# Sliding-window attention with a rational feed-forward: the order of all instructions planned by a list scheduler in the source

## Chip, cores and metric

The kernel runs on one core of one Trainium2 chip. The metric is the device time of one execution in microseconds (us), lower is better. Times named "span" run from the first to the last instruction of one profiled execution.

A core has five engines with a queue of instructions each: PE (matrix products, results into PSUM), DVE (vector operations), ACT (activation functions, copies), POOL (elementwise operations on SBUF) and SP (here it issues the DMAs). Each engine takes the instructions of its queue strictly in order; an instruction that waits for a semaphore holds all that stand behind it.

## What is computed

```python
# q, k, v: (8, 8, 576, 64);  window 64, scale 1/8
scores = scale * np.matmul(q, k.transpose(0, 1, 3, 2))
mask = (rel >= 0) & (rel < window)          # rel = row - column
attn = softmax(np.where(mask, scores, -1e9))
x = np.matmul(attn, v)                       # to (4608, 512)
h = x @ w_in                                 # w_in (512, 2048)
P = a[0] + a[1] * h + a[2] * h**2 + a[3] * h**3
Q = 1.0 + np.abs(b[0]) * np.abs(h) + np.abs(b[1]) * h**2
out = (P / (Q + 1e-6)) @ w_out               # w_out (2048, 512)
```

All in float32. The weights arrive as 8-byte words and are decoded on the chip.

## The kernel before

**Tiling.** The 4608 tokens are cut into 12 chunks of 384 (CH). The 2048 hidden columns are cut into 16 tiles of 128. A step (c, i) handles hidden tile i of chunk c; there are 192 steps. Each float32 product is split into three products of a shorter format (high and low parts of weights and data).

**A step** has an f1 product, `ffn1` up to L258: 4 blocks of the model width times 3 products, 12 matmuls of 128x384 into an `h` buffer of PSUM (2 buffers). Then the gate, L265 to L278: ACT makes `ah`, `num`, `u` from h; DVE multiplies `num` by h twice (L268, L269, the last readers of h); POOL multiplies `u` by `ah` (L270); ACT takes logarithm and exponential for 1/Q (L273, L274); DVE makes the high part `gh` and, with three more operations, the low part `gl` (L275 to L278). So DVE has six operations a gate, ACT five, POOL one. The temporaries `ah`, `u`, `num` have 2 buffers each, `gh` and `gl` four (LAG + 1). Last comes the output product, `ffn2`, L298: 9 matmuls of 128x512 into the three accumulators o0, o1, o2 of the chunk, issued LAG = 3 steps after the f1 product.

**Phases.** Steps run as chunk 0 tiles 0 to 7, chunk 1 tiles 0 to 7, chunk 1 tiles 8 to 15, chunk 0 tiles 8 to 15, and then chunks 2 to 11 with all 16 tiles. The first half of chunk 0's output is parked in `part` (L305) and added in L310.

**Weights.** `decode` (L110 to L133) turns one 512 KB tile into its high and low part: a DMA into `w_st` (3 buffers), ACT (L124), POOL (L127), DVE (L128, L129), ACT (L132), DVE (L133), with `w_c` in 2 buffers. There are 16 tiles of w_in and 16 of w_out.

**Attention.** Each chunk has four units, one for each pair of heads. `unit_load` issues the DMAs of q, k, v (L160 to L166); `unit_scores` makes the scores on PE (L200, 24 small matmuls; for chunks 1 and 2, PEM, the mask is added on PE, L193), masks on DVE (L211), takes the maximum (L207 or L214), exponentials on ACT (L218 or L221, six each with its sum), the reciprocal of the sums on DVE (L223, L224), and the normalisation (L225), on DVE for chunk 0 and on POOL for the others. `unit_transpose` transposes on PE (L232) into the same single PSUM tile `ps_s` that the scores use, and ACT copies to `pT` (L234). `unit_av` multiplies with v on PE (L243) into `ps_x` and makes the parts xh (ACT, L248) and xl (DVE, L249) of x, the input of the f1 products. q, kt, vt and `sm` have 2 buffers each.

**What sets the order.** The source emits the prologue (the four units of chunk 0 with four tiles of w_in between them), and then, step by step, the decodes due at that step, the f1 product and gate, the attention calls due, and the output product of three steps before. Tables say at which step a decode or a unit is due: the units of a chunk are spread over the phase ahead of it. This emission order is only a priority: the tile framework reorders the instructions with its own scheduler and cost model (`schedule_with_timeline_sim=True`) before it fixes each engine's queue.

Of the kernel before, what the change touches and what calls it, by code (L numbers as in the profile page):

```python
# [26 lines left out]
QADD = 1.0 + 1e-6  # L27


@with_exitstack  # L30
def swa_rational_ffn(ctx: ExitStack, tc: tile.TileContext, qT, kT, v, w_in, w_out, a, b, out):
# [121 lines left out]
    def unit_load(c, hp):  # L153
        q = kv.tile([P, TC, WIN], F32, name="q")
        kt = kv.tile([P, TC + 1, WIN], F32, name="kt")
        vt = kv.tile([P, TC, P], F32, name="vt")
        kw, vw, first = [], [], None
        j = kb = vb = 0
        for bi, t0, n in segments(c):
            nc.sync.dma_start(out=q[:, j:j + n, :].rearrange("p t s -> p (t s)"),  # L160
                              in_=qT[bi, hp, :, t0 * WIN:(t0 + n) * WIN])
            k0 = max(t0 - 1, 0)
            nw = n if t0 else n - 1
            nc.sync.dma_start(out=kt[:, kb:kb + nw + 1, :].rearrange("p t s -> p (t s)"),
                              in_=kT[bi, hp, :, k0 * WIN:(k0 + nw + 1) * WIN])
# [12 lines left out]
        m0 = None if first is None else MASKS[first]
        live[c, hp] = dict(q=q, kt=kt, vt=vt, kw=kw, vw=vw, m0=m0)

    def unit_scores(c, hp):
        u = live[c, hp]

        ps = ps_a.tile([P, 2, 512], F32, name="ps_s", bufs=1)
        m0 = u["m0"]
        on_pe = c in PEM
        if m0 is None:
            mm = mask[:, 1:2, :].broadcast_to([P, PR, P])
        else:
            mm = mask[:, m0:m0 + PR, :]  # L190
        if on_pe:
            for z in range(2):
                nc.tensor.matmul(ps[:, z, 0:PR * P].rearrange("p (r c) -> p r c", c=P), ident_r, mm, start=True, stop=False)  # L193
        for p in range(PR):
            for z in range(2):
                for e in range(2):
                    j = 2 * p + e
                    k = u["kt"][z * 64:z * 64 + 64].rearrange("p t s -> p (t s)")
                    w = u["kw"][j] * WIN
                    nc.tensor.matmul(ps[e * 64:e * 64 + 64, z, p * P:(p + 1) * P], u["q"][z * 64:z * 64 + 64, j, :],  # L200
                                     k[:, w:w + P], start=not on_pe, stop=not on_pe or p == PR - 1)
        sm = att.tile([P, 2 * PR, P], F32, name="sm")
        NR = 2 * PR
        nmx = att.tile([P, NR], F32, name="nmx")
        if on_pe:
            pss = ps[:, :, 0:PR * P].rearrange("p z (r c) -> p z r c", c=P)
            nc.vector.tensor_reduce(out=nmx.rearrange("p (z r) -> p z r", z=2), in_=pss, axis=AX.X, op=ALU.max, negate=True)  # L207
            nc.vector.scalar_tensor_tensor(out=nmx, in0=nmx, scalar=SCALE, in1=zero, op0=ALU.mult, op1=ALU.add)
        else:
            for z in range(2):  # L210
                nc.vector.scalar_tensor_tensor(out=sm[:, z * PR:(z + 1) * PR, :],  # L211
                                               in0=ps[:, z, 0:PR * P].rearrange("p (r c) -> p r c", c=P), scalar=SCALE,
                                               in1=mm.bitcast(F32), op0=ALU.mult, op1=ALU.add)
            nc.vector.tensor_reduce(out=nmx, in_=sm, axis=AX.X, op=ALU.max, negate=True)  # L214
        sums = att.tile([P, NR], F32, name="sums")
        for j in range(NR):
            if on_pe:
                nc.scalar.activation(sm[:, j, :], ps[:, j // PR, (j % PR) * P:(j % PR + 1) * P], AF.Exp, scale=SCALE,  # L218
                                     bias=nmx[:, j:j + 1], accum_out=sums[:, j:j + 1])
            else:  # L220
                nc.scalar.activation(sm[:, j, :], sm[:, j, :], AF.Exp, bias=nmx[:, j:j + 1], accum_out=sums[:, j:j + 1])  # L221
        rs = att.tile([P, NR], F32, name="rs")
        nc.vector.scalar_tensor_tensor(out=sums, in0=sums, scalar=1e-9, in1=zero, op0=ALU.add, op1=ALU.add)  # L223
        nc.vector.reciprocal(out=rs, in_=sums)  # L224
        (nc.vector if c < 1 else nc.gpsimd).tensor_tensor(out=sm, in0=sm, in1=rs.unsqueeze(2).broadcast_to([P, NR, P]), op=ALU.mult)  # L225
        u["sm"] = sm

    def unit_transpose(c, hp):
        u = live[c, hp]
        ps = ps_a.tile([P, 2, 512], F32, name="ps_s", bufs=1)  # L230
        for j in range(2 * PR):
            nc.tensor.transpose(ps[:, j // PR, (j % PR) * P:(j % PR + 1) * P], u["sm"][:, j, :], ident)  # L232
        pT = att.tile([P, 2, PR * P], F32, name="pT", bufs=1)
        nc.scalar.copy(out=pT, in_=ps[:, :, 0:PR * P])  # L234
        u["pT"] = pT

    def unit_av(c, hp):
        u = live.pop((c, hp))

        ps = ps_a.tile([P, TC, WIN], F32, name="ps_x", bufs=1)  # L240
        for j in range(TC):
            for z in range(2):
                nc.tensor.matmul(ps[z * 64:z * 64 + 64, j, :], u["vt"][:, u["vw"][j], z * 64:z * 64 + 64],  # L243
                                 u["pT"][:, z, j * WIN:(j + 1) * WIN], start=True, stop=True)
        xh[c, hp] = xp.tile([P, CH], F32R, name=f"xh{hp}")
        xl[c, hp] = xp.tile([P, CH], F32R, name=f"xl{hp}")
        x = ps.rearrange("p t s -> p (t s)")
        nc.scalar.copy(out=xh[c, hp], in_=x)  # L248
        nc.vector.tensor_tensor(out=xl[c, hp], in0=x, in1=xh[c, hp].bitcast(F32), op=ALU.subtract)  # L249

    gs = {}

    def ffn1(c, i):
        h = ps_h.tile([P, CH], F32, name="h")
        n = 0
        for cc in range(NCC):
            for w, x in ((wi_h, xl), (wi_h, xh), (wi_l, xh)):
                nc.tensor.matmul(h, w[:, cc, i * P:(i + 1) * P], x[c, cc], start=n == 0, stop=n == 3 * NCC - 1)  # L258
# [150 lines left out]
```

## Time and profile before

| what | value |
|---|---|
| median of 3 runs | 1013.71 us (1013.44 to 1014.66) |
| span of the profiled execution | 1014.7 us |
| busy: PE, DVE, ACT, POOL | 94%, 81%, 71%, 32% of the span |
| PE, DVE busy in 0 to 175 us | 120.9 us, 153.3 us |
| PE busy in 175 to 1000 us | 825.0 us |
| mean granted TensorE clock | 0.971 |

How to read the lines. In the busy time by stretch, each row gives the stretch, its length, and for each engine the busy time and the number of instructions in brackets; then the granted TensorE clock (1.00 is full speed), the busy share of the DMA engines and GB/s. In the groups of instructions, a row gives the source line, engine, operation, output and inputs, shapes, count, busy time in us and mean ns of one, and after the bar the idle time of the engine ahead of them with what ended it. In the order of time, a row gives start and duration in us; a bracket at its end names the idle time before it and what released it. PEld is the weight load of PE.

### The profile page before, as it was taken

How to read it: one execution, taken by the hardware profiler on the slowest of the kernel's cores; microseconds unless marked ns; L12 is line 12 of the kernel's file. 1: busy time of each engine (PE TensorE's matmuls, PEld its weight loads, DVE VectorE, ACT ScalarE, POOL GpSimd, SP SyncE). 2: the span in 40 equal slices, each digit the busy share in tenths (PEclk: the TensorE clock that was granted, in tenths of full speed). 3: DMA queues.
4: the chain of work that ended last, by engine and by line, in shares of the span. 5: the costliest groups of instructions: out<-in, count | busy, mean ns of one | idle time of the engine just before them, and what ended most of it. 6: DMA issues, size and time to landing. Idle time of an engine off the chain costs nothing.

```text
span 1014.7 us, 18277 instructions
## 1 busy us (share of the span) xinstructions
PE 954.8 (94%) x6640; PEld 844.8 (83%) x6640; DVE 825.9 (81%) x1539; ACT 725.1 (71%) x1735; POOL 324.9 (32%) x283
## 2 busy tenths in 40 slices
PE   3688578999999999999999999999999999999997
PEld 2576367989898888898888888888988988988996
DVE  7899788878888788788788787787787888787885
ACT  5777666667676777877777777777777777777664
POOL 4566544223332222223223223223223223222221
PEclk9679789999999999999999999999999999999999
DMA  7634630021211211210211211110121111100000
GB/s 239 221 110 138 207 98 16 1 77 29 90 31 31 83 42 34 88 37 29 76 46 31 67 58 34 64 61 29 61 61 31 62 63 35 64 17 1 32 1 31
DMA packets 37817, 64.09 MB, mean 63 GB/s; under 512 B 4448, under 2 KB 24928, under 8 KB 37728
## 3 DMA queue, kind: packets, MB, share of 16 engines
q1 hardware_dynamic: 37728, 62.93, 19.4%
q8 instruction: 52, 0.85, 0.4%
q14 instruction: 37, 0.30, 0.1%
HBM read 53.48 MB, written 9.44 MB: 62 GB/s over the span
## 4 chain that ended last, share of the span: by engine, by line
PE 84%; DVE 10%; ACT 3%; issue 2%; POOL 1%; DMA 1%; SPq 0%; POOLq 0%; DVEq 0%
PE h L258 38%; PE o L298 37%; PE ps_x L243 3%; PE ps_s L200 3%; PE ps_s L232 3%; DVE w_c L128 2%; POOL w_st L127 1%; DVE w_c L129 1%; DVE wo_l L133 1%; DVE num L277 1%; DVE u L276 1%; DVE wi_l L133 1%; DVE gh L275 1%; DMA w_st<-w_in 1%; ACT w_c L124 0%
## 5 line engine op out<-in xcount | busy, mean ns | idle before, releaser
L270 POOL TENSOR_TENSOR u<-u,ah 128x384 f32<-128x384 f32 x192 | 198.2, 1033 | 383.3 <-ACT u L267 343.7
L258 PE MATMUL h<-xl,wi_h 128*128 128x384 f32 x768 | 267.5, 348 | 20.3 <-DVE num L269 18.6
L258 PE MATMUL h<-xh,wi_h 128*128 128x384 f32 x768 | 262.7, 342 | 0.0
L258 PE MATMUL h<-xh,wi_l 128*128 128x384 f32 x768 | 262.5, 342 | 0.0
L298 PE MATMUL o<-wo_h,gl 128*128 128x512 f32 x576 | 233.5, 405 | 7.2 <-DVE gl L278 7.2
L298 PE MATMUL o<-wo_h,gh 128*128 128x512 f32 x576 | 228.3, 396 | 0.0
L298 PE MATMUL o<-wo_l,gh 128*128 128x512 f32 x576 | 227.0, 394 | 0.0
L268 DVE TENSOR_TENSOR num<-num,h 128x384 f32<-128x384 f32 x192 | 106.2, 554 | 111.9 <-ACT num L266 111.5
L265 ACT ACTIVATE ah<-h 128x384 f32<-128x384 f32 x192 | 94.5, 492 | 124.1 <-PE h L258 84.9
L258 PEld LDWEIGHTS h<-xl,wi_h 128*128 128x128 f32 x768 | 147.3, 192 | 27.8 <-DVE num L269 20.7
L258 PEld LDWEIGHTS h<-xh,wi_h 128*128 128x128 f32 x768 | 147.4, 192 | 4.8
L225 POOL TENSOR_TENSOR sm<-sm,rs 128x768 f32<-128x768 f32 x44 | 68.4, 1555 | 253.2 <-DVE rs L224 250.5
L258 PEld LDWEIGHTS h<-xh,wi_l 128*128 128x128 f32 x768 | 147.0, 191 | 0.6 <-issue 0.2
L275 DVE SCALAR_TENSOR_TENSOR gh<-num,a_sb,ah 128x384 fp32r<-128x384 f32 x192 | 119.3, 633 | 28.4 <-ACT ah L274 28.3
L298 PEld LDWEIGHTS o<-wo_h,gl 128*128 128x128 f32 x576 | 109.0, 189 | 33.7 <-DVE gl L278 8.8
L267 ACT ACTIVATE u<-ah,b_sb 128x384 f32<-128x384 f32 x192 | 135.6, 707 | 0.0
L221 ACT ACTIVATE sm<-sm,nmx 128x128 f32<-128x128 f32 x240 | 93.3, 390 | 57.4 <-DVE nmx L214 57.4
L298 PEld LDWEIGHTS o<-wo_h,gh 128*128 128x128 f32 x576 | 109.3, 190 | 25.2
L266 ACT ACTIVATE num<-h,a_sb 128x384 f32<-128x384 f32 x192 | 128.3, 668 | 0.0
L298 PEld LDWEIGHTS o<-wo_l,gh 128*128 128x128 f32 x576 | 109.2, 190 | 18.5
L269 DVE SCALAR_TENSOR_TENSOR num<-num,a_sb,h 128x384 f32<-128x384 f32 x192 | 117.7, 614 | 6.1
L277 DVE SCALAR_TENSOR_TENSOR num<-num,a_sb,u 128x384 f32<-128x384 f32 x192 | 116.7, 622 | 0.4
(52 smaller groups left out, 1139.2 us busy)
## 6 DMA issues: line engine op xcount, KB each, us to landing
out<-ob SPq DMA_DIRECT2D x33, 256.0 KB, 2.5
w_st<-w_in SPq DMA_DIRECT2D x16, 512.0 KB, 3.7
w_st<-w_out SPq DMA_DIRECT2D x16, 512.0 KB, 4.2
q<-qT SPq DMA_DIRECT2D x32, 192.0 KB, 3.2
vt<-v SPq DMA_DIRECT2D x16, 384.0 KB, 3.1
vt<-v SPq DMA_DIRECT2D x16, 320.0 KB, 3.0
kt<-kT SPq DMA_DIRECT2D x16, 224.0 KB, 3.6
kt<-kT SPq DMA_DIRECT2D x16, 192.0 KB, 3.4
```

Source lines behind the costliest of these rows:

```text
L221: nc.scalar.activation(sm[:, j, :], sm[:, j, :], AF.Exp, bias=nmx[:, j:j + 1], accum_out=sums[:, j:j + 1])
L225: (nc.vector if c < 1 else nc.gpsimd).tensor_tensor(out=sm, in0=sm, in1=rs.unsqueeze(2).broadcast_to([P, NR, P]), op=ALU.mult)
L258: nc.tensor.matmul(h, w[:, cc, i * P:(i + 1) * P], x[c, cc], start=n == 0, stop=n == 3 * NCC - 1)
L265: nc.scalar.activation(ah, h, AF.Abs)
L266: nc.scalar.activation(num, h, AF.Identity, scale=a_sb[:, 3:4], bias=a_sb[:, 2:3])
L267: nc.scalar.activation(u, ah, AF.Identity, scale=b_sb[:, 1:2], bias=b_sb[:, 0:1])
L268: nc.vector.tensor_tensor(out=num, in0=num, in1=h, op=ALU.mult)
L269: nc.vector.scalar_tensor_tensor(out=num, in0=num, scalar=a_sb[:, 1:2], in1=h, op0=ALU.add, op1=ALU.mult)
L270: nc.gpsimd.tensor_tensor(out=u, in0=u, in1=ah, op=ALU.mult)
L275: nc.vector.scalar_tensor_tensor(out=gh, in0=num, scalar=a_sb[:, 0:1], in1=ah, op0=ALU.add, op1=ALU.mult)
L277: nc.vector.scalar_tensor_tensor(out=num, in0=num, scalar=a_sb[:, 0:1], in1=u, op0=ALU.add, op1=ALU.subtract)
L298: nc.tensor.matmul(acc[c][t], g[:, ts], w[:, i, :], start=first and n == 0, stop=last and n == 2)
```

## The change

The functions above are taken apart into operations, each a small function bound to one engine, with a planned cost, a rank, the operations it comes after, and the buffer slots it uses. A class `Plan` holds them all. Its method `order` simulates the five engines: again and again it takes, over all engines, the operation that can start earliest, and among those of one engine that can start within 0.02 us of one another the one of lowest rank. A handover between engines costs 0.15 us in the plan. A buffer slot is free when its last user has ended. The operations are then emitted in the order of their planned starts, inside `tc.manual_schedule()`, so that the framework keeps this order.

What the diff changes beside that:

- Ranks: a unit of chunk 0 has -12 to -9, a unit of another chunk the step at which its phase's predecessor begins plus a quarter phase for each unit, minus AHEAD = 3; w_in tile i has the step that first needs it minus 1.5, a w_out tile that step plus LAG minus 1.5; a gate its step; an output product its step plus LAG + 0.5.
- Units are tied to one another only kind by kind (scores after scores, transposes after transposes, values after values).
- q and k are loaded by one operation, v by another.
- The normalisation of chunk 0 moves from DVE to POOL.
- x has two fixed sets of buffers, and a chunk's x waits for the last f1 product of the set's former holder.
- The last outputs go through the `w_st` buffers instead of `part`.
- The loads of the coefficients a and b are emitted ahead of everything in the plan.

```diff
+class Plan:
+    LATENCY = 0.15
...
+    def order(self):
...
+            for e in ENGINES:
+                able = []
+                for op in ready[e]:
+                    if any(not slots[s.pool] for s in op.takes):
+                        continue
+                    t = max([free[e], op.ready] + [min(slots[s.pool]) for s in op.takes])
+                    able.append((t, op))
...
+                t0 = min(t for t, _ in able)
+                t, op = min(((t, op) for t, op in able if t <= t0 + 0.02), key=lambda x: (x[1].rank, x[0]))
+                if best is None or t < best[0]:
+                    best = t, op
...
+        return sorted(self.ops, key=lambda o: o.start)
...
+    plan = Plan({"w_st": 3, "w_c": 2, "qk": 2, "vt": 2, "sm": 2, "pT": 1, "ps_s": 1, "ps_x": 1, "h": 2, "tmp": 2, "gp": LAG + 1,
+                 "o0": 1, "o1": 1, "o2": 1, "x": NCH})
...
+        o = plan.add("SP", 2.3, rank - 2, load, uses=[st])
+        o = plan.add("ACT", 0.57, rank, scale, [o], [st, sc])
+        o = plan.add("POOL" if pool_sign else "ACT", 1.8 if pool_sign else 0.57, rank, sign, [o], [st])
+        o = plan.add("DVE", 0.62, rank, put_sign, [o], [st, sc])
+        o = plan.add("DVE", 0.62, rank, put_low, [o], [st, sc])
+        o = plan.add("ACT", 0.56, rank, high, [o], [sc])
+        return plan.add("DVE", 0.62, rank, rest, [o], [sc])
...
+        r = lambda n: rank + 0.03 * n
+        o = link("load_qk", plan.add("SP", 1.9, r(0) - 2, load_qk, [], [sqk]))
+        lv = link("load_v", plan.add("SP", 1.8, r(0) - 1.9, load_v, [], [svt]))
+        o = link("scores", plan.add("PE", 1.36 if on_pe else 1.0, r(1), scores, [o, chain.get("scores")], [sqk, ssm, sps]))
+        if not on_pe:
             for z in range(2):
+                o = plan.add("DVE", 0.47, r(2), lambda z=z: masked(z), [o], [ssm, sps])
+        o = plan.add("DVE", 1.15 if on_pe else 0.87, r(3), maxima, [o], [ssm, sps] if on_pe else [ssm])
+        o = plan.add("ACT", 2.1, r(4), exps, [o], [ssm, sps] if on_pe else [ssm])
+        o = plan.add("DVE", 0.45, r(5), invert, [o])
+        o = plan.add("POOL", 1.6, r(6), normalise, [o], [ssm])
+        o = link("transposes", plan.add("PE", 0.7, r(7), transposes, [o, chain.get("transposes")], [ssm, spt]))
+        o = plan.add("ACT", 0.75, r(8), copy_pT, [o], [spt, spT])
+        o = plan.add("PE", 0.95, r(9), values, [o, lv, chain.get("values")], [svt, spT, spx])
...
+        r = lambda n: s + 0.05 * n
+        f = f1[s] = plan.add("PE", 2.09, s, products, x_ready[c] + [tile_in[i], f1.get(s - 1)], [sh])
+        a0 = plan.add("ACT", 0.42, r(1), absolute, [f], [sh, st])
+        n0 = plan.add("ACT", 0.58, r(2), num0, [a0], [sh, st])
+        u_0 = plan.add("ACT", 0.61, r(3), u0, [a0], [st])
+        n1 = plan.add("DVE", 0.47, r(4), num1, [n0], [sh, st])
+        n2 = plan.add("DVE", 0.53, r(5), num2, [n1], [sh, st])
+        u_1 = plan.add("POOL", 1.05, r(5), u1, [u_0], [st])
...
+        g = plan.add("DVE", 0.54, r(8), g_high, [o, n2], [st, sg])
+        o = plan.add("DVE", 0.5, r(9), product, [g], [st, sg])
+        o = plan.add("DVE", 0.53, r(10), remainder, [o], [st])
+        gate_done[s] = plan.add("DVE", 0.47, r(11), g_low, [o], [st, sg])
...
+            o = plan.add("PE", 0.695, s + LAG + 0.5 + 0.01 * t, lambda t=t: products(t),
+                         [gate_done[s], tile_out[i], f2.get((s - 1, t)), f2.get((s, t - 1))], [sg, so[t]])
...
+        tile_in[i] = plan_decode(w_in[i], wi_h[:, :, sl], wi_l[:, :, sl], need[i] - 1.5, True)
+        tile_out[i] = plan_decode(w_out_v[:, i, :], wo_h[:, i, :], wo_l[:, i, :], need[i] + LAG - 1.5, True)
...
+                order.append((c, k, -12 + k if c == 0 else before + (prev // NU) * k - AHEAD))
...
+    load_coefficients()
+    with tc.manual_schedule():
+        for op in plan.order():
+            op.emit()
```

More of the change, by code (lines that the diff above doesn't have):

```diff
@@ L30, in swa_rational_ffn @@
+ENGINES = "PE", "DVE", "ACT", "POOL", "SP"
 @with_exitstack
@@ L228, in unit_transpose @@
[L228 to L249, printed above, removed]
@@ L291, in ffn2 @@
         last = s == total - 1 or steps[s + 1][0] != c
+        d, sg = gs.pop(s)
         if first:
-            acc[c] = [ps_o.tile([P, DO], F32, name=f"o{t}") for t in range(NTS)]
-        gh, gl = gs.pop((c, i))
-        for t in range(NTS):
-            ts = slice(t * P, (t + 1) * P)
-            for n, (g, w) in enumerate(((gl, wo_h), (gh, wo_l), (gh, wo_h))):
-                nc.tensor.matmul(acc[c][t], g[:, ts], w[:, i, :], start=first and n == 0, stop=last and n == 2)
-        if not last:
-            return
@@ new lines, in products, with store @@
+        def products(t):
+            if first:
+                acc[t] = ps_o.tile([P, DO], F32, name=f"o{t}")
+            ts = slice(t * P, (t + 1) * P)
+            for n, (g, w) in enumerate(((d["gl"], wo_h), (d["gh"], wo_l), (d["gh"], wo_h))):
+                nc.tensor.matmul(acc[t], g[:, ts], w[:, i, :], start=first and n == 0, stop=last and n == 2)
+        def store(t, e):
+            if spill:
+                if t == 0:
+                    part[c] = const.tile([P, NTS, DO], F32, name=f"part{c}")
+                nc.scalar.copy(out=part[c][:, t, :], in_=acc[t])
+                return
+            ob = e["ob"] = stage.tile([P, DO], F32, name="ob", tag="w_st", bufs=3)
+            if merge:
+                nc.vector.tensor_tensor(out=ob, in0=acc[t], in1=part[c][:, t, :], op=ALU.add)
+            else:
+                nc.scalar.copy(out=ob, in_=acc[t])
@@ new lines, in swa_rational_ffn @@
+    seen = []
+    for c, i0, i1 in phases:
+        if c not in seen:
+            before = begin[c] - prev
+            for k in range(NU):
+                order.append((c, k, -12 + k if c == 0 else before + (prev // NU) * k - AHEAD))
+            seen.append(c)
+        prev = i1 - i0
+    last_step = {}
+    for s, (c, i) in enumerate(steps):
+        last_step[c] = s
+    holder = {}
+    n = 0
+    s = 0
+    for c, k, rank in order:
+        if c >= C0 and k == 0:
+            old = max(x for x in range(c) if slot_of[x] == slot_of[c])
+            while s <= last_step[old]:
+                plan_gate(s)
+                s += 1
+            free_x[c] = [f1[last_step[old]]]
+        plan_unit(c, k, rank)
```

461 lines of the change are left out of this document (296 added, 165 removed).

## The prediction

> **What bounds the kernel now.** I read the page first, then busy time by stretch, then the f1 products by stretch, then the waits of the first 175 us, and the order of time in three places.
>
> ```profile
> span 1014.7 us, 18277 instructions
> PE 954.8 (94%) x6640; PEld 844.8 (83%) x6640; DVE 825.9 (81%) x1539; ACT 725.1 (71%) x1735; POOL 324.9 (32%) x283
> ```
> ```profile
> core 0: us, PE busy (x) PEld busy (x) DVE busy (x) ACT busy (x) POOL busy (x), PEclk, DMA share, GB/s
> 0.00:25.00 25.00, 8.51 (x108) 6.67 (x108) 17.46 (x32) 13.59 (x41) 11.42 (x20) 0.99 0.73 237
> 25.00:100.00 75.00, 58.02 (x416) 49.26 (x417) 71.50 (x117) 55.67 (x141) 43.88 (x26) 0.80 0.51 161
> 100.00:125.00 25.00, 14.25 (x136) 10.84 (x134) 19.91 (x34) 14.92 (x35) 13.84 (x8) 0.77 0.61 189
> 125.00:175.00 50.00, 40.15 (x233) 34.49 (x234) 44.44 (x74) 34.26 (x89) 23.68 (x17) 0.88 0.22 69
> 175.00:1000.00 825.00, 825.00 (x5720) 737.23 (x5719) 667.46 (x1278) 602.25 (x1426) 231.07 (x212) 1.00 0.14 45
> ```
>
> There are three stages. From 175 to 1000 us PE is busy for all 825 us: whatever the order of the other engines, nothing is to be won there, only lost. Before 175 us PE works 8.5 + 58.0 + 14.3 + 40.2 = 120.9 us and idles 54.1, part of it at a low granted clock; DVE works 17.5 + 71.5 + 19.9 + 44.4 = 153.3 us and idles 21.7. So DVE bounds the start. What follows 1000 us is taken up in part 3. The end is the moment at which PE is saturated plus the PE work left then. The position of PE at the start is counted by f1 products (12 matmuls a step), that of DVE by the gh operation (one a step):
>
> ```profile
> 0.00:175.00 175.00, 50.05 (x204) 44.34 (x204) 0.84 0.47 149
> 175.00:203.00 28.00, 15.21 (x83) 14.70 (x84) 1.00 0.00 1
> ...
> 0.00:175.00 175.00, 11.79 (x15) 0.84 0.47 149
> 175.00:203.00 28.00, 4.95 (x8) 1.00 0.00 1
> ```
>
> The first two rows are line L258, the last two L275. At 175 us PE has done 204/12 = 17 products, at 203 us (204 + 83)/12 = 24, with 15 and 23 gates behind them. Yet all 32 weight tiles are decoded by 175 us (the L129 row below), although the second half of w_in is first needed from step 16 to step 23, one tile a step. The scheduler of before filled DVE with decodes ahead of their need, and what PE needed came late. Its worst place is around 110 us:
>
> ```profile
> 107.00 0.69 DVE L133 SCALAR_TENSOR_TENSOR wi_l<-w_c,wi_h 128x512 fp32r<-128x512 f32 x1
> ...
> 111.91 1.96 DVE L129 SCALAR_TENSOR_TENSOR w_c<-w_st,w_c 128x512 uint32<-128x512 uint32 x1
> 111.61 1.72 POOL L225 TENSOR_TENSOR sm<-sm,rs 128x768 f32<-128x768 f32 x1 [1.52 <-DVE rs L224]
> 113.38 0.90 PE L232 MATMUL ps_s<-ident,sm 128*128 128x128 f32 x3 [5.37 <-POOL sm L225]
> ```
>
> PE waits 5.4 us for the last attention unit of chunk 1, without which step 8 cannot be computed, while DVE decodes tiles. The waits of the first 175 us say the same of the gates (total, times, longest): a product waits for an h buffer that DVE has not yet read.
>
> ```profile
> PEld h L258 <- DVE num L269: 20.7, 7, 6.2
> ```
>
> **Part 1, the order of the start (gain).** The number of instructions does not change, and phases and steps are the same (eight steps of chunk 0, eight of chunk 1, then the second halves). What changes is who goes first. Units of chunk 0 get ranks -12 to -9, units of chunk 1 -3 to 3, a w_in tile the step that needs it minus 1.5, a w_out tile plus 1.5, a gate its step. So attention goes ahead of decodes, and a decode goes ahead of a gate only when it is due. To bring PE to step 24 the DVE needs, beside the 153.3 us of the first 175, eight more gates (15 to 23).
>
> ```profile
> L129 DVE SCALAR_TENSOR_TENSOR w_c<-w_st,w_c 128x512 uint32<-128x512 uint32 x32 | 26.0, 814 | 0.2
> L275 DVE SCALAR_TENSOR_TENSOR gh<-num,a_sb,ah 128x384 fp32r<-128x384 f32 x15 | 11.8, 786 | 3.1 <-ACT ah L274 3.0
> L268 DVE TENSOR_TENSOR num<-num,h 128x384 f32<-128x384 f32 x17 | 9.2, 545 | 0.7 <-ACT num L266 0.7
> L225 DVE TENSOR_TENSOR sm<-sm,rs 128x768 f32<-128x768 f32 x4 | 4.3, 1070 | 0.1
> ```
>
> A gate has six DVE operations; these are the longest and the shortest, 786 and 545 ns, so a gate costs between 6 x 0.545 = 3.3 and 6 x 0.666 = 4.0 us; durations overlap a little at their ends, so I take 3.5: 28 us. The four normalisations of chunk 0 (L225, 4.3 us) leave DVE for POOL. They don't leave it free: beside the POOL row at 111.61 the DVE operation at 111.91 took 1.96 us where its like at 107.00 took 0.69. Four such blocks cost 4 x 1.3 = 5 us, so the move is worth between -4.3 and +0.7 us; I take -2, since a block needs a two-input operation just behind it. POOL itself has room (43.9 us busy of 75). DVE then needs 153.3 + 28 - 2 = 179 us, and step 24 comes at 179 plus the DVE idle time. If idle stays at 21.7, that is 201 us against 203: a gain of 2. The first 25 us alone hold 25 - 17.5 = 7.5 us, the wait for the first loads and scores, and they can't go: 186.5, a gain of 16. I take 12 us: always the most urgent of the ready operations goes, so DVE should seldom be without one, but the plan's prices lie below the rows (0.47 to 0.54 us for a gate's operations, 0.62 for the decode's 0.81), and a queue that runs behind its plan waits. That is 191 us, **gain 12**. The two coefficient loads now stand ahead of the first q on SP's queue and not behind the second w_st; at 0.7 us an issue (below) the first scores come up to 1.4 us later, which I leave within those 12.
>
> ```profile
> 4.60 0.71 SPq L89 DMA_DIRECT2D a_sb<-a  x1
> ```
>
> The Trainium skill, SBUF — State Buffer, section on the two separate sides, says that GpSimd and a DVE instruction with two SBUF inputs hold a shared port exclusively, the second blocking until the first is done. By that rule the moved normalisations give DVE nothing back, and the sum would end 2 us later; the row at 111.91 agrees with it.
>
> **Part 2, the steady stage (loss).** PE has no idle time to hide anything, so each added switch of PE counts in full. Before, the value products of a unit (L243) stand directly ahead of the scores of the next (L200); that is so 36 times in PE's order of time. The rows show the first such place and the last, and then one where the values stand alone:
>
> ```profile
> 234.90 0.34 PE L258 MATMUL h<-xh,wi_l 128*128 128x384 f32 x1
> 235.17 0.92 PE L243 MATMUL ps_x<-pT,vt 128*64 128x64 f32 x24
> 236.02 0.89 PE L200 MATMUL ps_s<-kt,q 64*64 64x128 f32 x24
> 236.83 0.50 PE L298 MATMUL o<-wo_h,gl 128*128 128x512 f32 x1
> 237.17 0.40 PE L298 MATMUL o<-wo_l,gh 128*128 128x512 f32 x1
> ...
> 907.55 0.92 PE L243 MATMUL ps_x<-pT,vt 128*64 128x64 f32 x24
> 908.40 0.86 PE L200 MATMUL ps_s<-kt,q 64*64 64x128 f32 x21
> ...
> 214.91 0.92 PE L243 MATMUL ps_x<-pT,vt 128*64 128x64 f32 x24
> 215.76 0.51 PE L298 MATMUL o<-wo_h,gl 128*128 128x512 f32 x1
> 216.10 0.40 PE L298 MATMUL o<-wo_l,gh 128*128 128x512 f32 x1
> ```
>
> Matmuls of L258 follow one another at 0.175 us, those of L298 at 0.23 (the rows of the end, below, are two of each). Going in costs 235.17 - 234.90 - 0.175 = 0.10 us, coming out 237.17 - 236.83 - 0.23 = 0.11, the same where the values stand alone (216.10 - 215.76 - 0.23 = 0.11); between values and scores nothing shows, their 24 take 0.85 us in all three places. In the new order the units of a chunk have ranks four steps apart. A unit's chain from scores to values is 8.4 us of planned work and seven handovers of 0.15 us, some 12 us with queueing (an estimate), while four steps of 4.2 us and the unit's own 2.6 are 19. So values and the next scores stand apart: 36 x 0.2 = **7 us more**.
>
> The second cost is in-order waiting. The plan puts a unit's transposes on PE as soon as it expects the normalisation to be done, since their rank is below that of the steps. Before, PE came 3.5 us after the normalisation's end (418.76 to 422.28):
>
> ```profile
> 417.29 1.47 POOL L225 TENSOR_TENSOR sm<-sm,rs 128x768 f32<-128x768 f32 x1 [6.40 <-DVE rs L224]
> 422.28 0.82 PE L232 MATMUL ps_s<-ident,sm 128*128 128x128 f32 x6
> ```
>
> With that slack gone, the piece of PE work under way covers the rest, 0.7 us for a third of an output product and 2.09 for an f1 product. If the chain runs later than planned, PE stands still with ready products queued behind it. Over 40 units that is between 0 and, at half a microsecond each, 20 us; most planned costs agree with the rows, so I take 0.05 us a unit, **2 us**. Gates (three steps of lag, four gh buffers), loads and the output copies keep more than a step of slack; I cost them at nothing. Splitting q/k from v moves only issues on SP's queue, which runs two units ahead.
>
> **Part 3, the end (gain).**
>
> ```profile
> 1000.25 0.34 PE L258 MATMUL h<-xh,wi_h 128*128 128x384 f32 x1
> 1000.42 0.33 PE L258 MATMUL h<-xh,wi_l 128*128 128x384 f32 x1
> 1004.38 0.39 PE L298 MATMUL o<-wo_l,gh 128*128 128x512 f32 x1
> 1004.61 0.40 PE L298 MATMUL o<-wo_h,gh 128*128 128x512 f32 x1
> 1007.27 0.50 PE L298 MATMUL o<-wo_h,gl 128*128 128x512 f32 x1 [2.26 <-DVE gl L278]
> 1010.51 0.63 PE L298 MATMUL o<-wo_h,gh 128*128 128x512 f32 x1
> ```
>
> Before works in pairs of steps: after the last f1 product two output products are left to cover its gate (1000.6 to 1005.0), PE idles 2.26 us, and the last output product, nine matmuls, takes 1010.51 + 0.63 - 1007.27 = 3.9 us, at a falling clock, instead of 9 x 0.23 = 2.1. The new order alternates f1 of a step with the output product of three steps earlier, so three products (6.2 us) cover a gate of 6.5 us (1000.75 to 1007.27). Idle falls to 0.3 us and the clock stays: 2.0 + 1.8, **gain 4** (2 if the clock falls all the same).
>
> Sum: 1014.7 - 12 + 7 + 2 - 4 = 1007.7 us for the profiled span. That span lies 1.0 above the median of the runs (1013.71), so I predict 1006.7, rounded 1007.
>
> **The rivals.** First, slower: PE stalls at the transposes of each unit. For it: planned slack falls from 3.5 us to below one PE piece, and PE is the bound. Against: the gaps between DVE, ACT and POOL are in the plan with 0.15 us each, about what the rows show. At 0.4 us over 40 units it costs 16 instead of 2: 1007 + 14 = 1021. It decides against the change from about 0.23 us a unit. Second, the start packs almost fully: the idle time falls to the 7.5 us of the head and the gates cost 3.3 us (gain 18), the stalls are nil and the values still meet the next scores: 1014.7 - 18 - 4 - 1.0 = 992 us. For it: 21.7 us of DVE idle and decodes far ahead of need. Third, the start gains nothing: in-order queues make DVE wait for late gates with decodes queued behind them, and only 7 + 2 - 4 remain: 1019 us. For it: PE's granted clock is 0.77 to 0.88 from 25 to 175 us, while the plan has 2.09 us for a product. Fourth, the change doesn't do what it says, the framework's order standing in the main: 1014.
>
> **How the numbers follow.** Forecast 0.45, stalls 0.20, full packing 0.17, no gain at the start 0.12, no change 0.06. The range for 8 in 10 takes in the first rival at 1021, with 2 us for the bound of the end, and the second at 992: 992 to 1023. Both signs are in it; the likeliest case alone holds 1000 to 1013. About 0.2% (2 us) is what a measurement of this kernel can tell from no change. Faster: 0.45 x 0.95 + 0.17 + a little = 0.61. Within: 0.10, from no change and the edges of two cases. Slower: 0.29.
>
> **What would show it.** Right: PE's first fully busy stretch begins with step 24 near 190 us, no wait of PE for POOL sm at the end of chunk 1's attention, L243 and L200 apart from 230 us on, 0.8 us more PE time a chunk, PE idle below 1 us ahead of the last product. Wrong: PE idle time in the middle stage put down to POOL sm or ACT pT (first rival), step 24 at 200 us or more (third), L243 still followed by L200 (no split).

## The result, and the profile after

The change made the kernel slower: 1116.49 us (1116.20 to 1116.85, 4 runs) against 1013.62 us (1013.44 to 1014.66, 4 runs), a ratio of 1.1008 with a 95% interval of 1.0992 to 1.1023. The head of the page after:

```profile
span 1114.8 us, 18288 instructions
PE 975.6 (88%) x6640; PEld 831.2 (75%) x6640; DVE 957.1 (86%) x1535; ACT 732.3 (66%) x1735; POOL 337.0 (30%) x287
```

The number of operations hardly changed, yet DVE is busy 131 us longer (825.9 before). 101 us of this are operations that take longer; the other 30 come from operations that follow one another with less overlap at their ends. Where the span grew is seen by counting f1 products, 12 matmuls each. Busy time by stretch of the f1 line alone (stretch, length, busy time with the count of matmuls, granted clock, DMA share, GB/s), before (L258) and then after (L470):

```profile
0.00:169.20 169.20, 47.80 (x192) 0.84 0.49 154
169.20:203.30 34.10, 17.77 (x96) 1.00 0.00 1
203.30:243.20 39.90, 18.12 (x98) 1.00 0.21 67
243.20:896.20 653.00, 306.67 (x1632) 1.00 0.16 51
```
```profile
0.00:150.00 150.00, 37.54 (x193) 0.97 0.42 133
150.00:215.00 65.00, 20.92 (x96) 0.87 0.32 102
215.00:259.80 44.80, 18.25 (x97) 1.00 0.16 51
259.80:992.50 732.70, 307.60 (x1632) 1.00 0.15 46
992.50:1114.80 122.30, 55.54 (x288) 1.00 0.04 14
```

The stretches were cut at steps 16 (192 matmuls), 24, 32 and 168. Step 16 came 19 us earlier than before (150 for 169), step 24 was 12 us late (215 for 203), step 32 was 17 us late (260 for 243). The 136 steps up to 168 (1632 matmuls), 8.5 times a chunk of 16, took 732.7 us for 653.0: 86.2 us a chunk for 76.8. The rest took 122.3 us for 118.5. So 80 of the 100 us were lost in the stage where PE had been saturated. Busy time by stretch of all engines, to be held against the prediction's first table:

```profile
0.00:25.00 25.00, 10.72 (x132) 8.54 (x132) 9.56 (x20) 10.71 (x34) 9.26 (x19) 1.00 0.51 179
175.00:1000.00 825.00, 745.16 (x5166) 639.96 (x5167) 709.39 (x1155) 551.08 (x1317) 229.27 (x196) 0.99 0.16 50
```

PE now idles 80 us of these 825, while DVE is busier with fewer instructions (709.4 us and 1155 for 667.5 and 1278). The waits (total, times, longest) name what PE, and ACT, waited for:

```profile
PE ps_s L411 <- POOL sm L406: 71.0, 38, 5.8
ACT ah L476 <- DVE gl L515: 52.8, 61, 1.6
PE h L470 <- DVE num L488: 12.0, 14, 2.2
```

The transposes (L411) wait for the normalisation 38 times in 48 units, 1.9 us each. POOL, which the line names, is only the last link of that chain. Three groups of DVE, before and then after, show an earlier one:

```profile
L277 DVE SCALAR_TENSOR_TENSOR num<-num,a_sb,u 128x384 f32<-128x384 f32 x192 | 116.7, 622 | 0.4
L276 DVE SCALAR_TENSOR_TENSOR u<-u,gh 128x384 f32<-128x384 f32 x192 | 105.3, 563 | 6.1
L278 DVE TENSOR_TENSOR gl<-num,ah 128x384 fp32r<-128x384 f32 x192 | 105.1, 559 | 1.8
```
```profile
L506 DVE SCALAR_TENSOR_TENSOR u<-u,gh 128x384 f32<-128x384 f32 x192 | 158.1, 823 | 22.0 <-DVE gh L502 0.9
L510 DVE SCALAR_TENSOR_TENSOR num<-num,a_sb,u 128x384 f32<-128x384 f32 x192 | 147.9, 771 | 5.5
L488 DVE SCALAR_TENSOR_TENSOR num<-num,a_sb,h 128x384 f32<-128x384 f32 x192 | 118.0, 615 | 6.8
L515 DVE TENSOR_TENSOR gl<-num,ah 128x384 fp32r<-128x384 f32 x192 | 130.5, 680 | 5.1
```

The same operations on the same shapes keep DVE busy 109 us more (158.1 + 147.9 + 130.5 for 105.3 + 116.7 + 105.1). By the means it is 102 us, since before some of them overlapped in pairs. L488, whose second input h lies in PSUM, keeps the 608 to 615 ns that it has in all the variants below. The order of time shows what runs beside the slow ones:

```profile
409.49 1.01 POOL L492 TENSOR_TENSOR u<-u,ah 128x384 f32<-128x384 f32 x1 [2.46 <-ACT u L482]
409.57 1.34 DVE L506 SCALAR_TENSOR_TENSOR u<-u,gh 128x384 f32<-128x384 f32 x1
...
414.32 1.02 POOL L492 TENSOR_TENSOR u<-u,ah 128x384 f32<-128x384 f32 x1 [3.82 <-ACT u L482]
414.39 1.36 DVE L515 TENSOR_TENSOR gl<-num,ah 128x384 fp32r<-128x384 f32 x1
...
418.12 1.04 POOL L492 TENSOR_TENSOR u<-u,ah 128x384 f32<-128x384 f32 x1 [2.79 <-ACT u L482]
418.32 1.26 DVE L510 SCALAR_TENSOR_TENSOR num<-num,a_sb,u 128x384 f32<-128x384 f32 x1
```

A DVE operation that starts behind POOL's multiplication of u ends 0.4 us after POOL does (414.39 + 1.36 = 415.75, against 415.34), where it takes 0.56 us alone (e1, below): as if most of it were done after POOL's end. This is the block of the prediction's row at 111.91, now in the gates. Counted in the order of time, of the 576 operations of the three lines, 137 begin while a multiplication of u runs and take 1.26 to 1.35 us in the mean of their line; those that begin beside no POOL operation take 0.55 to 0.62. Before, one of the 576 began there. The Trainium skill, SBUF — State Buffer, section on the two separate sides, has the rule: a GpSimd operation that reads SBUF and a DVE operation with two SBUF inputs hold one port pair exclusively. The rows agree, and L488, which reads h from PSUM, is untouched: 31 times it begins beside a multiplication of u, and takes 0.615 us as elsewhere.

What this does to a unit, in the same stretch after:

```profile
416.29 0.89 PE L368 MATMUL ps_s<-kt,q 64*64 64x128 f32 x24
420.09 1.02 DVE L374 SCALAR_TENSOR_TENSOR sm<-ps_s,mask 128x384 f32<-128x384 f32 x2
425.74 1.59 POOL L406 TENSOR_TENSOR sm<-sm,rs 128x768 f32<-128x768 f32 x1 [6.57 <-DVE rs L402]
427.38 0.87 PE L411 MATMUL ps_s<-ident,sm 128*128 128x128 f32 x6 [1.65 <-POOL sm L406]
```

The scores end at 417.18, but the mask begins at 420.09, behind the gate operations in DVE's queue, the blocked L510 at 418.32 among them; the block alone adds 0.64 us (1.26 for 0.62). The plan has the transposes at the moment when the normalisation should be done, and PE stands still with ready products behind them.

### The profile page after: what moved, and what is told of

The parts are those of the page before. It is cut to its first block, busy times and chain, and to the rows that moved or that the text cites. A ratio compares the mean times of both kernels' runs of the same rounds, so it can differ in the third digit from the quotient of the medians.

```text
span 1114.8 us, 18288 instructions
## 1 busy us (share of the span) xinstructions
PE 975.6 (88%) x6640; PEld 831.2 (75%) x6640; DVE 957.1 (86%) x1535; ACT 732.3 (66%) x1735; POOL 337.0 (30%) x287
## 4 chain that ended last, share of the span: by engine, by line
DVE 68%; PE 11%; ACT 8%; POOL 6%; issue 5%; DVEq 1%; DMA 0%; POOLq 0%; SPq 0%; ACTq 0%
DVE u L506 13%; DVE num L510 12%; DVE gh L502 10%; DVE gl L515 9%; DVE num L488 6%; POOL sm L406 5%; DVE num L485 5%; PE o L553 4%; DVE nmx L385 3%; DVE sm L374 3%; PE h L470 3%; PE ps_s L411 3%; ACT pT L415 3%; DVE w_c L274 2%; DVE xl L430 2%
## 5 line engine op out<-in xcount | busy, mean ns | idle before, releaser
L492 POOL TENSOR_TENSOR u<-u,ah 128x384 f32<-128x384 f32 x192 | 204.3, 1064 | 465.7 <-ACT u L482 456.6
L470 PE MATMUL h<-xl,wi_h 128*128 128x384 f32 x768 | 263.6, 343 | 17.2 <-DVE num L488 12.0
L470 PE MATMUL h<-xh,wi_l 128*128 128x384 f32 x768 | 259.2, 337 | 2.9 <-DVE wi_l L290 2.9
L470 PE MATMUL h<-xh,wi_h 128*128 128x384 f32 x768 | 258.6, 337 | 0.0
L553 PE MATMUL o<-wo_h,gl 128*128 128x512 f32 x576 | 240.8, 418 | 17.6 <-ACT wo_h L287 12.1
L553 PE MATMUL o<-wo_l,gh 128*128 128x512 f32 x576 | 231.0, 401 | 10.6 <-DVE wo_l L290 10.5
L502 DVE SCALAR_TENSOR_TENSOR gh<-num,a_sb,ah 128x384 fp32r<-128x384 f32 x192 | 126.4, 658 | 83.9 <-ACT ah L498 70.7
L495 ACT ACTIVATE ah<-u 128x384 f32<-128x384 f32 x192 | 101.1, 526 | 142.1 <-POOL u L492 142.0
L506 DVE SCALAR_TENSOR_TENSOR u<-u,gh 128x384 f32<-128x384 f32 x192 | 158.1, 823 | 22.0 <-DVE gh L502 0.9
L470 PEld LDWEIGHTS h<-xl,wi_h 128*128 128x128 f32 x768 | 144.9, 189 | 39.4 <-DVE num L488 24.6
L406 POOL TENSOR_TENSOR sm<-sm,rs 128x768 f32<-128x768 f32 x48 | 76.4, 1592 | 270.7 <-DVE rs L402 246.3
L510 DVE SCALAR_TENSOR_TENSOR num<-num,a_sb,u 128x384 f32<-128x384 f32 x192 | 147.9, 771 | 5.5
L470 PEld LDWEIGHTS h<-xh,wi_h 128*128 128x128 f32 x768 | 145.0, 189 | 5.4
L470 PEld LDWEIGHTS h<-xh,wi_l 128*128 128x128 f32 x768 | 144.8, 189 | 4.4 <-DVE wi_l L290 4.4
L397 ACT ACTIVATE sm<-sm,nmx 128x128 f32<-128x128 f32 x240 | 93.2, 390 | 79.1 <-DVE nmx L385 79.1
L476 ACT ACTIVATE ah<-h 128x384 f32<-128x384 f32 x192 | 93.6, 488 | 70.2 <-DVE gl L515 52.8
L515 DVE TENSOR_TENSOR gl<-num,ah 128x384 fp32r<-128x384 f32 x192 | 130.5, 680 | 5.1
```

The costliest lines, as they stand in the source:

```text
L406: nc.gpsimd.tensor_tensor(out=sm, in0=sm, in1=u["rs"].unsqueeze(2).broadcast_to([P, NR, P]), op=ALU.mult)
L476: nc.scalar.activation(d["ah"], d["h"], AF.Abs)
L492: nc.gpsimd.tensor_tensor(out=d["u"], in0=d["u"], in1=d["ah"], op=ALU.mult)
L495: nc.scalar.activation(d["ah"], d["u"], AF.Ln, bias=QADD)
L502: nc.vector.scalar_tensor_tensor(out=d["gh"], in0=d["num"], scalar=a_sb[:, 0:1], in1=d["ah"], op0=ALU.add, op1=ALU.mult)
L506: nc.vector.scalar_tensor_tensor(out=d["u"], in0=d["u"], scalar=QADD, in1=d["gh"].bitcast(F32), op0=ALU.add, op1=ALU.mult)
```

## The experiments

Two theories at first. A: POOL's u runs beside DVE operations with two SBUF inputs, DVE falls behind its plan, and the in-order queues pass that on to PE. B: the plan leaves the transposes no slack, whatever DVE does. The columns: the start of steps 24 and 32, a chunk of 16 steps between steps 32 and 168, the rest from step 168 to the end, the profiled span, the median, and the kernel before on the same chip (all in us; the f1 products are counted in the order of time).

| kernel | 24 | 32 | chunk | rest | span | time | before |
|---|---|---|---|---|---|---|---|
| before | 203 | 243 | 76.8 | 118.4 | 1014.7 | 1013.6 | |
| after | 215 | 260 | 86.2 | 122.2 | 1114.8 | 1116.5 | 1013.6 |
| e1 | 201 | 242 | 79.1 | 113.0 | 1027.6 | 1029.4 | 1016.7 |
| e2 | 216 | 259 | 84.0 | 124.2 | 1097.3 | 1099.1 | 1016.7 |
| e3 | 206 | 244 | 77.2 | 115.2 | 1016.2 | 1018.0 | 1016.7 |
| e4 | 204 | 252 | 86.3 | 122.0 | 1107.2 | 1109.0 | 1016.7 |
| e5 | 225 | 270 | 85.0 | 128.5 | 1121.0 | 1123.3 | 1014.4 |
| e6 | 203 | 246 | 82.4 | 128.5 | 1074.3 | 1076.1 | 1014.4 |
| e7 | 248 | 293 | 86.0 | 119.7 | 1143.3 | 1145.1 | 1014.4 |
| e8 | 202 | 242 | 77.2 | 114.8 | 1012.3 | 1014.0 | 1014.4 |
| e9 | 209 | 250 | 77.6 | 112.9 | 1022.0 | 1022.1 | 1014.0 |
| e10 | 197 | 244 | 77.6 | 113.3 | 1017.7 | 1019.4 | 1014.0 |
| e11 | 197 | 245 | 78.3 | 112.3 | 1022.4 | 1023.4 | 1014.0 |
| e12 | 197 | 242 | 80.7 | 112.7 | 1040.6 | 1044.1 | 1013.8 |
| e13 | 204 | 244 | 77.5 | 112.7 | 1015.1 | 1015.7 | 1013.6 |
| e14 | 204 | 249 | 79.4 | 114.6 | 1038.2 | 1039.3 | 1013.6 |

e1 to e8 were timed once each; the others have an interval, given with them. All start from the kernel after.

**e1.**

```diff
-            nc.gpsimd.tensor_tensor(out=d["u"], in0=d["u"], in1=d["ah"], op=ALU.mult)
+            for half in range(2):
+                nc.gpsimd.memset(d["u"], 0.25)
```

> The gate's multiplication on POOL (L492) is replaced by two fills of u with a constant, so POOL reads nothing there; the product of u and ah is left out. Theory A (POOL's reads block DVE operations with two SBUF inputs, the gate runs past its plan, and PE is held by the two tmp buffers and the late chains): L506, L510 and L515 fall from 0.82, 0.77 and 0.68 to 0.56 to 0.62 us, a step of the last chunk falls from 4.4 to 4.2 us, the idle time ahead of the transposes falls from 71 us to under 35, the span to 1020 to 1050 us. Theory B (PE stalls only because the transposes stand without slack in its queue): DVE may get faster, but the transposes' waits stay above 60 us and the span above 1090 us.

Two of the DVE groups and the wait at the transposes in e1:

```profile
L507 DVE SCALAR_TENSOR_TENSOR u<-u,gh 128x384 f32<-128x384 f32 x192 | 110.6, 576 | 21.9 <-DVE gh L503 0.9
L516 DVE TENSOR_TENSOR gl<-num,ah 128x384 fp32r<-128x384 f32 x192 | 106.9, 557 | 5.1
```
```profile
PE ps_s L411 <- POOL sm L406: 15.3, 11, 5.8
```

POOL fills u twice, 0.84 us a gate for the 1.06 of the product, and reads no SBUF; the durations are back (576 for 823 ns, 557 for 680). That POOL is also 0.2 us faster here is a rival, which e9 below answers with the full product. The span falls by 87 of the 100 us: 18 at the start, 60 in the steady stage, 9 at the end. A chunk still takes 2.3 us more than before the change.

**e2 and e8.**

```diff
-                    o.ready = max(x.end + ...
+                    o.ready = getattr(o, "extra", 0.0) + max(x.end + ...
+        o.extra = 3.0
```

In the last line o is the transposes. e8 is e1 with this and 1 us for the values.

> In the plan alone, transposes count as ready 3 us later than the normalisation's end; nothing else changes. Theory B (no slack): the waits of PE for POOL sm go from 71 us to under 10, span 1030 to 1050 us. Theory A (blocked DVE and the two tmp buffers): the waits ahead of the transposes go, but PE then waits for h and gl, and a step stays at 4.4 us or more; span 1070 to 1100 us.

> No reads on POOL in the gate (fills, as in the first run, the product of u and ah left out), and in the plan transposes ready 3 us later and values 1 us later. If what is left in the first run beside the blocks (79.1 us a chunk against 76.85) is two thirds missing slack and one third the split of values and scores, a chunk falls to 77.6 to 78 us and PE has no idle time from 275 to 1000 us; span 1012 to 1022 us. If the slack is not the rest, a chunk stays at 79.

With the collisions in place the slack is worth 17 us, and the wait has moved one operation on, to the values (A had expected it at h and gl):

```profile
PE ps_x L421 <- ACT pT L415: 47.4, 39, 2.6
```

Without collisions it is worth 15 us (1027.6 to 1012.3), and PE is busy throughout:

```profile
275.00:1000.00 725.00, 725.00 (x5027) 643.93 (x5026) 609.53 (x1121) 536.76 (x1265) 178.21 (x340) 1.00 0.14 44
```

So B holds for 15 to 17 us, and A for the 87 that slack doesn't touch.

**e3.**

```diff
-    with tc.manual_schedule():
-        for op in plan.order():
-            op.emit()
+    for op in plan.order():
+        op.emit()
```

> The same plan, but emitted outside the manual schedule, so that the framework's own scheduler reorders with the planned order as priority. Theory A and B both lay the loss on the fixed order, so the time should return near that of before, 1000 to 1035 us, with pairs of gates and transposes some us after the normalisation. If something else in the changed kernel costs the time (the slots of x, the split loads, the normalisation of chunk 0 on POOL), it stays above 1080 us.

The same operations and buffers, put in order by the framework, take 1018.0 us. It brings the gates of two steps together, as before, and L506, L510 and L515 take 588, 637 and 575 ns. So the loss comes with the fixed order, not with the taking apart, the two sets of x or the moved normalisations.

**e4.**

```diff
-        tile_in[i] = plan_decode(..., need[i] - 1.5, True)
-        tile_out[i] = plan_decode(..., need[i] + LAG - 1.5, True)
+        tile_in[i] = plan_decode(..., need[i] - 5.5, True)
+        tile_out[i] = plan_decode(..., need[i] + LAG - 5.5, True)
```

> Weight tiles get ranks four steps earlier. Theory of the start (step 24 came at 215 us and not at 191, because PE stands waiting for tiles decoded just in time, 25 us of waits for wo_h, wo_l and wi_l): these waits fall below 10 us, step 32 comes at 240 to 250 us and not at 260, span 1098 to 1108 us. Rival (DVE is simply full in the start): step 16 comes as much later as steps 16 to 32 gain, span 1112 to 1120 us.

Step 24 comes 11 us sooner, step 32 8 us, the end 7.6 us, and a chunk is unchanged: the just-in-time weights cost 8 us of the start. Step 32 comes at 252, just outside the expected 240 to 250, and step 16 no later than in the change, which speaks against the rival.

**e5, e6, e7: three plain remedies.** In e5 the planner lets no POOL operation that reads SBUF overlap a DVE operation with two SBUF inputs. In e6 the multiplication of u is done by DVE (`nc.vector`, planned cost 0.5). In e7 `tmp` has three buffers for two and `w_c`, to make room, one.

```diff
+                    if getattr(op, "port", False):
+                        t = max(t, port["POOL" if e == "DVE" else "DVE"])
```

> Only the plan is changed: a POOL operation that reads SBUF and a DVE operation with two SBUF inputs may not overlap in it, so the fixed order keeps them apart as far as times hold. All work is done as in the changed kernel. Theory A (blocked DVE operations put the gates behind the plan): L506, L510 and L515 fall to 0.56 to 0.66 us, the waits ahead of the transposes fall below 40 us, span 1015 to 1050 us. If the loss lies in POOL's own time (two fills are also 0.1 to 0.2 us shorter than the product), it stays above 1080 us.

> The gate's multiplication moves from POOL to DVE, in the plan too, so POOL reads only for normalisations and decodes. Theory A: L506, L510 and L515 fall to their unblocked 0.56 to 0.62 us; DVE gets 0.5 us more a step but loses 0.56 us of blocking, so its busy time stays near 950 us and the gate chain is 0.5 to 1 us shorter: span 1030 to 1070 us, between no reads on POOL (1028) and the changed kernel (1115). Theory C (DVE's sum of busy time is what bounds, not the place of the blocks): no gain, 1100 us or more.

> Three buffers for the gate's temporaries in place of two, in the plan too; one w_c in place of two pays for the space, so the start gets slower by 10 to 40 us and is not compared. If the loop of two temporaries passes the blocks on to PE, a step of the last chunk falls from 4.4 to 4.2 us though L506 to L515 stay long, and a chunk of the steady stage from 86.2 us to 80 or less. If the block reaches PE by another way (DVE's order, the transposes without slack), the last chunk falls but the steady chunks stay above 84 us.

e5 is no better than the change. The waits at the transposes fall to 8.8 us, as A expected, but PE waits 58.2 us for h in their place, and the groups of DVE show that the collisions took place all the same (g_high, product and g_low; less in the remainder):

```profile
L514 DVE SCALAR_TENSOR_TENSOR u<-u,gh 128x384 f32<-128x384 f32 x192 | 164.2, 855 | 17.5 <-DVE gh L510 0.5
L510 DVE SCALAR_TENSOR_TENSOR gh<-num,a_sb,ah 128x384 fp32r<-128x384 f32 x192 | 151.6, 789 | 16.2 <-ACT ah L506 15.4
L523 DVE TENSOR_TENSOR gl<-num,ah 128x384 fp32r<-128x384 f32 x192 | 142.8, 744 | 6.1
```

A plan fixes the order and not the times: POOL starts when u is ready, not when the plan has it. So e5 doesn't tell what an order free of collisions would cost. e6 has none with u (574, 624 and 557 ns in the same three operations), but DVE carries 111 us of POOL's work (192 times 580 ns), and a chunk takes 82.4 us; its span, 1074.3, lies between what A and C expected. e7 leaves a chunk at 86.0: two sets of temporaries don't hold the steady stage up, though ACT's wait for gl (52.8 us) suggested it. Its start is worse by 33 us, with `w_c` the only thing that was made scarcer.

**e9 and e13: which DVE operations run beside POOL.**

```diff
-        n1 = plan.add("DVE", 0.47, r(4), num1, [n0], [sh, st])
-        n2 = plan.add("DVE", 0.53, r(5), num2, [n1], [sh, st])
+        n1 = plan.add("DVE", 0.47, r(4) - 1, num1, [n0], [sh, st])
+        n2 = plan.add("DVE", 0.53, r(5) - 1, num2, [n1], [sh, st])
```

> The full computation with one change to the planner: the two VectorE operations of a gate that read h from PSUM (L485 and L488) are ranked one step earlier, so that they go ahead of the late operations of the gate before and run while GpSimd multiplies u (L492). Theory A (what costs is that GpSimd's u runs beside VectorE operations with two SBUF inputs): the means of L506, L510 and L515, 823, 771 and 680 ns after the change, fall to 560 to 650 each, some 60 to 100 us of VectorE time go, a steady chunk takes 77.5 to 80 us in place of 86.2, and the span lies at 1025 to 1055. Theory B (the transposes lack slack in the plan, whatever VectorE does): nothing is added to their slack, so 1100 to 1115. Theory C (only that h is freed earlier): the 24.6 us of waits of L470 for L488 go and no more, 1090 to 1100.

> e1 (the product of u and ah left out, two fills in its place, so no collisions) with the reordering of e9. Theory A: e9 had gained 94 us where there were collisions; with none there is little left to gain, and a steady chunk stays at 78 to 79.1 us (e1: 79.1), the time at 1020 to 1030. Theory C (the order itself, by freeing h and starting the gate earlier): the chunk falls to 77 or below and the time to 1010 to 1018.

e9 takes 1022.1 us, 1.0077 (1.0055 to 1.0100) of before: two ranks brought back 94 of the 103 us. The order of time and three groups of e9:

```profile
403.52 0.61 DVE L488 SCALAR_TENSOR_TENSOR num<-num,a_sb,h 128x384 f32<-128x384 f32 x1
403.69 1.02 POOL L492 TENSOR_TENSOR u<-u,ah 128x384 f32<-128x384 f32 x1
...
409.73 1.01 POOL L492 TENSOR_TENSOR u<-u,ah 128x384 f32<-128x384 f32 x1 [5.02 <-ACT u L482]
409.93 0.61 DVE L488 SCALAR_TENSOR_TENSOR num<-num,a_sb,h 128x384 f32<-128x384 f32 x1
410.46 0.70 DVE L510 SCALAR_TENSOR_TENSOR num<-num,a_sb,u 128x384 f32<-128x384 f32 x1
```
```profile
L510 DVE SCALAR_TENSOR_TENSOR num<-num,a_sb,u 128x384 f32<-128x384 f32 x192 | 136.1, 709 | 3.7
...
L506 DVE SCALAR_TENSOR_TENSOR u<-u,gh 128x384 f32<-128x384 f32 x192 | 111.3, 579 | 19.9 <-DVE gh L502 0.5
L515 DVE TENSOR_TENSOR gl<-num,ah 128x384 fp32r<-128x384 f32 x192 | 108.3, 564 | 4.7
```

POOL's multiplication now lies beside L488, which is not blocked: 122 times of 192 L488 begins there, and takes 615 ns as elsewhere. Only L510 still catches its tail now and then, and its 709 ns miss what A expected. 81 us of DVE time are gone (436.5 to 355.7), inside A's range, and the span of 1022.0 is 3 us below A's. POOL's product takes 1.04 us here, so its length was not the cause. e13 separates the rival C (h is freed earlier): without collisions the same two ranks gain 13.7 us (1029.4 to 1015.7; 1.0019 of before, 1.0006 to 1.0033), where A had expected hardly anything. The time lies in C's range, the chunk of 77.5 between the two. So up to 14 us of the 94 are C's, and some 80 belong to the collisions, if the two add up.

**e10, e11, e12, e14: can the plan beat the kernel before?** e10 is e9 with 1 us of slack for the transposes and the weights two steps earlier. e11 emits the next unit's scores directly behind the values. e12 ties them in the plan:

```diff
-        ... scores, [o, chain.get("scores")], [sqk, ssm, sps]))
+        ... scores, [o, chain.get("scores"), chain.get("behind")], [sqk, ssm, sps]))
+        if chain.get("behind"):
+            chain["scores"].rank = chain["behind"].rank + 0.001
```

e14 is e9 with the slack of e8 (3 and 1 us) and the earlier weights.

> The full computation, with the reordering of e9, 1 us of slack for the transposes in the plan, and the weights ranked two steps earlier. If A is the main cause and B and the late weights the rest: a steady chunk at 77 to 78 us, step 24 at 204 to 210 us, span 1008 to 1035, TensorE waiting under 20 us in all in the middle. If A is wrong, 1085 to 1105, as a sum of what the slack (17 us for 3 us of it) and the earlier weights (8 us) gave alone.

> e10, with the scores of the next unit issued directly behind the values of one, as in the kernel before. If the split of the two costs what the prediction took (0.2 us for each of 36), 4 to 7 us less than e10; if TensorE's stalls hide it, or if the scores then wait for a buffer, within 3 us of e10 or up to 10 above it.

> The full computation: e10, and in the plan itself the scores of a unit now depend on the values of the unit before and are ranked right behind them, from the ninth unit on, so that the two run back to back as in the kernel before. Between 330 and 970 us TensorE left its large matmuls 63 times in the kernel before and 92 times in e10; here it should be 62 to 68. If each visit costs the 0.2 us that the prediction took, the steady chunk falls from 77.5 to 76.8 or 77.0 us, and the time from 1019.4 to 1012 to 1015: level with the kernel before or just under it. If the visits cost nothing, or if the chain makes the scores late (as in e11, where the moved scores brought back 6 us of stalls), 1018 to 1026.

> The full computation: the reordering of e9, in the plan 3 us of slack for the transposes and 1 us for the values (as in e8), the weights two steps earlier. Theory A with B: what e8 showed without collisions (chunk 77.1 us, 1014) comes back with the product in it, plus the early weights: chunk 77 to 77.7, step 32 at 240 to 245 us, 1008 to 1020. If the slack pushes gates and units onto each other again, as the chained scores did in e12 (1044), 1025 to 1045.

e10 is the best of the full computations in planned order: 1019.39 us, 1.0049 (1.0037 to 1.0062) of before. In its steady stage PE is busy throughout:

```profile
275.00:1000.00 725.00, 724.96 (x5009) 640.02 (x5008) 628.38 (x1117) 533.83 (x1263) 207.15 (x186) 1.00 0.14 44
```

Yet a chunk takes 0.8 us more than before. Between 330 and 970 us PE leaves its large matmuls for attention 92 times in e10 and 63 times before; 29 visits more, all of scores and values, in 640 us are 3.5 a chunk, at 0.2 us each 0.7 us. The traces with hardly any stalls bear this out. Between steps 32 and 168 PE makes 68 visits before, 102 in e13, and 84 in e8, where half the units keep values and scores together: e8 needs 3 us less than e13 and 3 more than before, 0.17 us a visit. e11 has 70 visits and e12 62, as meant, but both lose more than they gain, e12 far more than either case that it was to decide between: e11 1.0089 (1.0074 to 1.0105), with PE idle 6 us of the 725, and e12 1.0297 (1.0281 to 1.0313). In e12 the collisions partly return (the u and gl operations take 645 and 636 ns for 585 and 578 in e10), and so do waits:

```profile
PE ps_x L421 <- ACT pT L415: 20.2, 29, 3.1
```

e14 goes the same way (gl at 664 ns, PE waiting 27.1 us for h; 1.0252, 1.0237 to 1.0267), inside its second range. The returned collisions are small: the three operations take 364 us in e10, 380 in e12 and 371 in e14, for 436 in the change. What else in these orders holds PE wasn't followed operation by operation. No full computation in planned order came as low as the kernel before.

## Why the prediction was wrong

The forecast span was 1007.7 us, the measured one 1114.8. Of the 107.1 us between them, 70.7 fell in the steady stage (9 more forecast, 79.7 more measured), 28.6 before step 32 (12 less, 16.6 more) and 7.8 at the end (4 less, 3.8 more).

- **The step that failed** is the one in part 2 that set the gates at nothing, "three steps of lag, four gh buffers". That slack covers the output product, but not DVE's queue, in which the attention units stand behind the gates. And the prices were taken from operations as they ran in the order of before, where POOL's multiplication mostly lay elsewhere: 1 of the 576 operations of the three lines began beside it, and 51 of those that read h from PSUM. The prediction had the mechanism in hand, with its row, and applied it to the four moved normalisations (5 us) and not to the 192 multiplications of u, whose neighbours the new order changed as well. Measured: 102 to 109 us of DVE time, and 87 us of span by e1, some 80 by e9 and e13. Two of the prediction's own signs of being wrong showed: PE idle time put down to POOL sm, and step 24 after 200 us.
- **The waits at the transposes** were mis-sized as a consequence: 0.05 us a unit and 2 us in the sum, against 71.0 us over 38 waits. "Most planned costs agree with the rows" was true of each operation alone. The first rival was right in kind, but its 0.4 us a unit was under a quarter of what came. With the collisions gone, lost slack costs 15 us (e1 against e8), inside the stated bound of 0 to 20.
- **Part 1, gain 12: wrong.** PE was ahead at step 16, by 19 us, and behind at step 24. To step 24 DVE needed 184.9 us of work and 30.2 of idle time, not 179 and 12. The work is more through collisions (172.2 in e1). The idle time is not theirs: e1 has 28.9 us of it as well, and step 24 at 201. In the first 25 us alone DVE is busy 9.6 us where it had been busy 17.5, and does 2 operations of decodes for 12. The first decode on ACT, before and then after, shows why:

```profile
7.56 0.66 ACT L124 ACTIVATE w_c<-w_st 128x512 f32<-128x512 f32 x1 [2.87 <-DMA w_st<-w_in]
```
```profile
10.20 0.40 ACT L397 ACTIVATE sm<-sm,nmx 128x128 f32<-128x128 f32 x1 [4.86 <-DVE nmx L385]
...
16.99 1.24 ACT L263 ACTIVATE w_c<-w_st 128x512 f32<-128x512 f32 x2
```

The ranks put attention first, so the decode stands in ACT's queue behind the exponentials of two units, and those wait for DVE's maxima. The early decodes that the prediction called harmful had filled such time. e4 gets 8 us back by ranking them earlier, e10 reaches step 24 at 197. How much of the 30 us comes from this one queue wasn't settled.

- **The split, 7 us: right, in cause and size.** In e10 and e13, where PE doesn't wait, 0.8 and 0.7 us a chunk over 8.5 chunks are 6 to 7 us. The Trainium skill, TensorEngine Tiling (Array Packing), Key Properties, says that a change of tiling mode drains TensorE. The 0.2 us a visit of scores and values, which run in smaller modes (64\*64 and 128\*64 in their rows), agrees with it.
- **Part 3, gain 4: right in kind, and covered up.** After the change PE still idled ahead of the last two products, 2.75 us and not 0.3:

```profile
1105.03 0.50 PE L553 MATMUL o<-wo_h,gl 128*128 128x512 f32 x1 [1.30 <-DVE gl L515]
...
1108.82 0.51 PE L553 MATMUL o<-wo_h,gl 128*128 128x512 f32 x1 [1.45 <-DVE gl L515]
...
1110.77 0.40 PE L553 MATMUL o<-wo_h,gh 128*128 128x512 f32 x1
```

Without the blocks the forecast idle time came: 0.20 us in e1 and 0.35 in e9 ahead of the last product. The last nine matmuls took 2.35 us after the change, not the 3.9 of before, much as forecast (2.1). From step 168 to the end e1 and e9 need 113 us for 118.4, a gain of 5, where the change itself lost 4.

## What to carry to other kernels

An order is also a choice of what runs beside what. Before pricing a reordering, list the pairs of engines that block one another, and ask for every such operation, the moved and the unmoved, who its new neighbour is; a duration from the old trace holds for its old neighbours only. In a plan that is fixed ahead, slack for whatever holds the bounding engine is worth a trial and no rule: 3 us of it gained 15 to 17 us here, but in the order of e9 it lost time (e14 against e10). Try two ranks before new buffers or another engine: here two ranks were worth 94 of 103 us.

## What the runs showed that was not expected

- A blocked DVE operation loses most of the time that it overlaps: 0.56 to 0.63 us alone (means of e1), 1.26 to 1.36 us behind a multiplication of 1.0 us. The two operations that read one input from PSUM, L485 and L488, took 549 and 615 ns in e9, where they often run beside it, and 550 and 615 in e13, where POOL reads nothing in the gate.
- POOL filling the same buffer without reading SBUF (e1) blocks nothing: the product L507 takes 0.56 us both beside a fill and away from it.
- The framework's own order (e3) mostly avoids these pairs (32 of the 576 operations, for 137) although nothing in the source asks for it, and comes to 1018.0 us from the source that takes 1116.5 in planned order.
